# Block 1 of a linear-attention and SwiGLU kernel: its q turned by VectorE, its sums of h put off behind the next pair

## The chip, the cores and the metric

The kernel runs on one core of a Trainium2 chip. The metric is the time of one execution in device microseconds (us). In the profiles PE is TensorE (PEld is its weight load), DVE is VectorE, ACT is ScalarE, POOL is GpSimd and SP is SyncE, whose queue issues most of the DMAs.

## The reference

```python
q, k, v: (8, 8, 576, 64)        # batch, heads, sequence, head_dim, float32
kv  = einsum('bhsd,bhse->bhde', k, v)
out = einsum('bhsd,bhde->bhse', q, kv)
out = out / sqrt(mean(out * out, axis=-1) + 1e-6) * g_norm
x   = out.transpose(0, 2, 1, 3).reshape(4608, 512)
y   = (silu(x @ w_gate) * (x @ w_val)) @ w_out     # w_gate, w_val: 512 x 1536, w_out: 1536 x 512
```

The three weights arrive as 64-bit words, and the kernel rounds them to float32 itself.

## The kernel before

**Blocks.** The 4608 tokens are cut into nine blocks of 512 (BLK), and the loop over n takes one block at a time. `Att` makes a block's x: kv from k and v (`load_kv`, `kv`), q loaded and turned so that the head dimension lies on the partitions (`load_q`, `turn`, `turn_q`), the product of q and kv (`product`), the root (`root`), the scaling (`scale`), and x turned back (`turn_x`). `Ffn` multiplies it with the weights: `up` gives h, `down` multiplies h with w_out. The attention of block n + 1 runs in between the products of block n's `down`, by the table that `steps` returns.

**Fast matrix products.** All products but the first block's up go by a scheme with seven products of half-size matrices in place of eight (Strassen's in Winograd's form). Its products are numbered 1 to 7, and `multiply(p)` issues product p and then the additions in `after<p>`. They gather in PSUM banks: 1, 6, 7 and 4 in "b", 2 in "a", 5 and then 3 in "c" (`CHAIN`). `after7` adds bank "c" to the copy u3 on DVE; only when that is read may product 3 add into the same bank. PSUM has three buffers of "b", two of "c" and "m" and one of "a".

**The blocks differ.** Block 0 has a plain up (`plain_up`, line 1008), because the weights are still being loaded and rounded. Block 1's up is one level deep (`Up`, six pairs j of 128-wide column groups, line 551): each pair takes three differences of weights, made by POOL in `prepare` into buffers of the pool "t" (nine of them, 256 KB each). From block 2 on (DEEP) up is two levels deep (`Inner`, line 706), and its weight sums, the leaves, come from DRAM. Block 1 makes these leaves besides its own work: after each product `make(4)` takes up to four steps of `leaf_steps`, which are small DVE additions and, in between, DMAs on SP that write t buffers, r buffers and the one buffer xi to the DRAM tensors w. A t buffer comes free for POOL only when such a write has landed.

**Sums of h.** Products 5 and others of `down` need sums of h's quarters: `h_sums(j, k, engine)` makes s1 = a21 + a22 and then a21 = s1 - a11, in place in h. In block 0 `plain_end` makes them for all six pairs in two large DVE instructions (128x1536 elements). In block 1 `after3` of pair j makes them for that pair (128x256), behind two POOL multiplications that write h.

**Order of pairs in block 1.** `Up.sequence` interleaves a pair with the one before it, which it calls last: 1, 5, then 4 and 3 of last, then 6, 2, 7. So `after3` of pair j comes after product 3 of pair j, which runs between products 5 and 6 of pair j + 1; `after7` of pair j + 1 comes at that pair's end.

**q.** From block 3 on (TURNED) q is loaded by `load_quarters`: 32 DMAs put the 32-column quarters of each head on their own partitions, so that DVE's transpose of 32x32 squares (line 331) turns it. Before that, q is loaded in rows of 256 bytes and turned by PE in 16 transposes per block (line 337), copied from PSUM by ACT and DVE. Block 1's q lands in four t buffers, block 2's in two buffers of the pool "ld" (four of them, which also hold k, v and the raw weights).

**Around the change, in block 0.** After `plain_end` PE has the kv products of block 1, the 16 transposes of its q, product 1 of block 0's down, block 1's first q product, product 5, product 6, and so on. POOL makes nine differences of w_out (`turn_t`, line 112) in t buffers for products 5, 7 and 4. The order on every engine comes from a list scheduler that follows the order of the program and the dependences; `tc.issue_after(x)` holds what is issued within it behind instruction x in that order. Each engine, and SP's queue, works through its list in order.

Of the kernel before, what the change touches and what calls it, by code (L numbers as in the profile page):

```python
# [8 lines left out]
F32 = mybir.dt.float32  # L9
# [5 lines left out]
P = 128  # L15
# [3 lines left out]
def kernel(  # L19
# [41 lines left out]
    nc = tc.nc  # L61
# [5 lines left out]
    BLK = P * T  # L67
# [5 lines left out]
    NP = NF // 2  # L73
    KT = 9
    LD = 2 * KT * D
# [4 lines left out]
    def pool(name, bufs, **kw):  # L80
        return ctx.enter_context(tc.tile_pool(name=name, bufs=bufs, **kw))

    consts = pool("consts", 1)
    ld_pool = pool("ld", 4)
# [26 lines left out]
    add = lambda e, o, a, b: e.tensor_tensor(out=o, in0=a, in1=b, op=OP.add)  # L111
# [3 lines left out]
    def ring():  # L115

        return r_pool.tile([P, 4, BLK], F32, name="r")

    class Words:
# [12 lines left out]
        def __init__(self, src, shape):  # L132
            self.raw = ld_pool.tile([P, LD], U32, name="ld")[:, 0 : 2 * BLK]
            dst = self.raw.rearrange("p (a b) -> p a b", a=shape[0])
            self.sent = nc.sync.dma_start(out=dst, in_=src)
            self.shape = shape
            self.begun = False
# [55 lines left out]
    class Att:  # L193


        def __init__(self, n):
            self.n = n

            self.cut, half = divmod(n, 2)
            self.split = half * D  # L200
            self.ps, self.z = {}, None
            self.q, self.k, self.v, self.room = [], {}, {}, None
            self.halves = []

        def parts(self, t):

            n, first = self.n, P * t - D * self.n
            if t < self.cut:
                return [(n - 1, S + first, 0, P)]
            if t == self.cut and self.split:  # L210
                return [(n - 1, S - D, 0, D), (n, 0, D, P)]
            return [(n, first, 0, P)]
# [73 lines left out]
            self.q.append(ld)  # L286

        def load_q(self, i):
            if self.n >= TURNED:
                self.load_quarters(i)  # L290
                return
            if self.n == 1:
                tiles = [t_tile().rearrange("p a b -> p (a b)") for _ in range(2)]
            else:
                ld = ld_pool.tile([P, LD], F32, name="ld")
                tiles = [ld[:, 0:BLK], ld[:, BLK : 2 * BLK]]
            for t in range(2):
                tile_ = tiles[t].rearrange("p (h d) -> p h d", h=H)
                for b, s0, p0, p1 in self.parts(2 * i + t):
                    nc.sync.dma_start(  # L300
                        out=tile_[p0:p1], in_=q[b, :, s0 : s0 + p1 - p0, :].rearrange("h p d -> p h d")
                    )
                self.q.append(tile_.rearrange("p (j u) d -> p j (u d)", u=2))
# [21 lines left out]
        def turn_q(self, i, pools=None):  # L325

            if i == 0:
                self.qt = ring().rearrange("p j (t c) -> p t j c", t=T)
            if self.n >= TURNED:
                to = self.qt[:, :, 2 * i : 2 * i + 2].rearrange("p t j c -> p j t c")  # L330
                nc.vector.transpose(out=to.rearrange("p j t c -> p (j t c)"), in_=self.q[i])
                return
            for t in (2 * i, 2 * i + 1):
                pool = pools[t % 2] if pools else m_psum
                ps = pool.tile([P, NS, P], F32, name=pool.name[0])
                for j in range(NS):
                    nc.tensor.transpose(ps[:, j], self.q[t][:, j], ident)
                if t % 2 if self.n == 0 else t:
                    self.copied_q = nc.scalar.copy(out=self.qt[:, t], in_=ps)
                else:  # L340
                    nc.vector.tensor_copy(out=self.qt[:, t], in_=ps)
# [186 lines left out]
    TURNED = 3  # L528
# [44 lines left out]
    class Up(Quad):  # L573
# [25 lines left out]
        def after7(self):  # L599
            self.u3 = self.piece(2)  # L600
            copied = nc.scalar.copy(out=self.u3, in_=self.ps["b"])

            with tc.issue_after(copied.ins):
                nc.scalar.activation(out=self.s, in_=self.s, func=ACT.Silu)
            add(nc.vector, self.u3, self.ps["c"], self.u3)

        def after4(self):
            g = self.piece(3)
# [3 lines left out]
        def after3(self):  # L612
            add(nc.vector, self.u2, self.ps["c"], self.u2)
            mul(nc.gpsimd, self.h[:, :, 0:HB], self.s, self.u2)
            self.ffn.ended = self.ffn.h_sums(self.j, 1, nc.vector)

        def multiply(self, p):
            super().multiply(p)
# [183 lines left out]
    def t_tile(key=None):  # L802

        stream.held.append(key)
        return t_pool.tile([P, 2, 2 * P], F32, name="t")
# [114 lines left out]
    class Ffn:  # L920
        def __init__(self, n, att):
            self.n, self.att = n, att
            self.h = h_pool.tile([P, NF, BLK], F32, name="h")
            self.ps, self.leaf_room, self.ended = {}, None, None

            self.making, self.later, self.latest = [], [], []

# [45 lines left out]
        def down(self, nxt):  # L973

            down = self.down_
            fill = nxt.steps() if nxt else {}
            for p in (1, 6, 5, 7, 2, 4, 3) if 5 in fill else (1, 5, 6, 7, 2, 4, 3):
                if p == 1:
                    down.turn_t(7, self.ended)
                if p == 6:  # L980
                    down.turn_t(4, nxt.halves[0] if nxt and nxt.n >= TURNED else None)
                down.multiply(p)
                self.make(12)
                if p == 5 and self.n == DEEP - 1:
                    for i in range(2):
                        self.loads(i)
                if p in fill:
                    fill[p]()
                if p in (1, 7) and self.latest:

                    with tc.issue_after(nxt.scaled.ins):
                        for step in self.latest.pop(0):
                            step()
                if p == 1:
                    down.turn_s3()

# [57 lines left out]
    for n in range(NB):  # L1056
        ffn = Ffn(n, blocks[n])
        nxt = blocks[n + 1] if n + 1 < NB else None
# [84 lines left out]
```

## Time and profile before

| | us |
|---|---|
| median of 8 runs (1035.22 to 1036.97) | 1035.71 |
| the profiled execution | 1035.98 |
| its span, first to last instruction | 1034.2 |
| PE busy | 1014.4 |
| PEld busy | 904.7 |
| DVE busy | 695.9 |
| POOL busy | 368.5 |
| ACT busy | 231.9 |
| granted TensorE clock, share of full | 1.00 |

The stages by PE's lines: attention of block 0 to about 35 us; block 0's plain up to 114; kv products, transposes of q and block 0's down to 160; block 1's up to 240; block 1's down to 282; then two-level blocks. Line 111 is the helper `add`, 112 `sub`, 113 `mul`, so these are read by their tiles (h, s, xi, t, r). In a timeline row the columns are start, duration, engine, line, operation, output and input tile with shapes, count, and in brackets the idle time before it with what ended it. A row of waits has the sum, the number and the longest. A row of the chain has start, duration and who carried it.

### The profile page before, as it was taken

Reading aid. Unit: us, or ns where it says so; the run is one execution under the profiler, and the core shown is the slowest. Engines: PE = TensorE matmul, PEld = TensorE weight load, DVE = VectorE, ACT = ScalarE, POOL = GpSimd, SP = SyncE. Lnnn points to the kernel's source line nnn. Section 1 sums busy time; section 2 is a strip of 40 time slices with the busy share of each in tenths; the row PEclk is TensorE's granted clock in tenths of the full one; section 3 lists DMA queues with packets and bytes.
Section 4 is the critical chain, followed back from the end, with each engine's and each line's share of the span. In section 5 each row is a group of like instructions: output and inputs, shape, how many; then the busy total and the mean of one; then the engine's idle time right before and its main releaser. Section 6 shows DMA issues by size and latency. Waiting matters only on the chain.

```text
span 1034.2 us, 21447 instructions
## 1 busy us (share of the span) xinstructions
PE 1014.4 (98%) x8586; PEld 904.7 (87%) x8586; DVE 695.9 (67%) x1184; ACT 231.9 (22%) x362; POOL 368.5 (36%) x280
## 2 busy tenths in 40 slices
PE   5999999999999999999999999999999999999998
PEld 4544688878899989998999899988999899989997
DVE  2999596886756855586666666674669466856661
ACT  2765121122221211212111112111212111211110
POOL 0000443334025612463156305640455136513670
PEclk9999999999999999999999999999999999999999
DMA  8689704773678457855686468736862766067601
GB/s 221 204 258 268 138 1 127 188 200 84 192 207 249 101 120 211 242 140 113 182 247 169 66 202 242 198 54 183 239 197 52 168 196 193 22 159 212 189 29 42
DMA packets 247876, 168.15 MB, mean 163 GB/s; under 512 B 124640, under 2 KB 215904, under 8 KB 247776
## 3 DMA queue, kind: packets, MB, share of 16 engines
q1 hardware_dynamic: 221280, 163.36, 57.7%
q10 hardware_dynamic: 26432, 3.41, 2.1%
q8 instruction: 68, 1.11, 0.4%
q14 instruction: 32, 0.26, 0.1%
q0 software_dynamic: 64, 0.00, 0.0%
HBM read 138.02 MB, written 22.41 MB: 155 GB/s over the span
## 4 chain that ended last, share of the span: by engine, by line
PE 90%; DVE 5%; DMA 3%; issue 1%; SPq 1%; ACT 1%; DVEq 0%; ACTq 0%
PE b L706 26%; PE b L551 20%; PE c L706 13%; PE c L551 9%; PE a L706 6%; PE a L551 5%; PE b L1008 4%; PE c L1008 4%; PE m L316 1%; PE m L357 1%; DVE r L112 1%; DMA h<-in_v_dram 1%; DVE xi L112 1%; DVE t L111 1%; DVE r L111 1%
## 5 line engine op out<-in xcount | busy, mean ns | idle before, releaser
L111 POOL TENSOR_TENSOR r<-r 128x256 f32<-128x256 f32 (+1 forms) x105 | 110.9, 1063 | 310.4 <-DVE r L111 263.1
L111 DVE TENSOR_TENSOR r<-b,r 128x512 f32<-128x512 f32 (+1 forms) x273 | 162.1, 606 | 64.9 <-PE b L706 59.6
L112 POOL TENSOR_TENSOR t<-wo 128x512 f32<-128x512 f32 x81 | 115.4, 1449 | 193.5 <-DVE wo L111 104.7
L111 DVE TENSOR_TENSOR r<-c,r 128x512 f32<-128x512 f32 (+1 forms) x179 | 108.5, 618 | 94.7 <-PE c L706 55.5
L706 PE MATMUL b<-x,t 128*128 128x128 f32 x1092 | 151.1, 275 | 0.0
L706 PEld LDWEIGHTS b<-x,t 128*128 128x128 f32 x1092 | 136.5, 192 | 0.7 <-DVE r L111 0.2
L111 DVE TENSOR_TENSOR r<-a,r 128x512 f32<-128x512 f32 (+1 forms) x99 | 62.5, 631 | 106.6 <-PE a L551 62.9
L706 PE MATMUL c<-xi,t 128*128 128x128 f32 x840 | 112.2, 275 | 0.4 <-DVE xi L111 0.4
L113 POOL TENSOR_TENSOR h<-r 128x1024 f32<-128x1024 f32 (+1 forms) x40 | 81.2, 2046 | 82.6 <-DVE r L111 77.1
L706 PEld LDWEIGHTS c<-xi,t 128*128 128x128 f32 x840 | 102.8, 192 | 0.5 <-DVE xi L111 0.5
L551 PE MATMUL b<-wo,h 128*128 128x256 f32 x432 | 99.4, 382 | 0.1
L551 PE MATMUL b<-t,h 128*128 128x256 f32 x432 | 96.9, 381 | 0.0
L551 PEld LDWEIGHTS b<-t,h 128*128 128x128 f32 x432 | 81.3, 190 | 11.3 <-issue 0.2
L551 PEld LDWEIGHTS b<-wo,h 128*128 128x128 f32 x432 | 79.9, 190 | 12.7 <-DVE h L113 2.5
L720 ACT COPY r<-b 128x512 f32<-128x512 f32 x63 | 36.9, 586 | 212.1 <-PE b L706 205.3
L706 PE MATMUL b<-xi,t 128*128 128x128 f32 x588 | 79.9, 276 | 0.0
L706 PEld LDWEIGHTS b<-xi,t 128*128 128x128 f32 x588 | 72.4, 192 | 0.1
L706 PE MATMUL b<-x,wg 128*128 128x128 f32 x336 | 52.7, 279 | 0.2 <-DVE x L112 0.2
L706 PE MATMUL b<-x,wv 128*128 128x128 f32 x336 | 51.3, 275 | 0.0
L551 PE MATMUL c<-t,s 128*128 128x256 f32 x216 | 48.3, 380 | 0.0
L551 PE MATMUL a<-wo,h 128*128 128x256 f32 x216 | 48.3, 379 | 0.0
L551 PE MATMUL c<-wo,h 128*128 128x256 f32 x216 | 48.1, 379 | 0.0
(136 smaller groups left out, 1573.8 us busy)
## 6 DMA issues: line engine op xcount, KB each, us to landing
t<-w SPq DMA_DIRECT2D x336, 256.0 KB, 3.5
out_dram<-r SPq DMA_DIRECT2D x17, 512.0 KB, 3.1
ld<-in_k_dram SPq DMA_DIRECT2D x26, 288.0 KB, 4.7
ld<-in_v_dram SPq DMA_DIRECT2D x26, 288.0 KB, 5.6
ld<-in_moe_w_gate_dram SPq DMA_DIRECT2D x12, 512.0 KB, 4.8
ld<-in_moe_w_val_dram SPq DMA_DIRECT2D x12, 512.0 KB, 4.7
ld<-in_moe_w_out_dram SPq DMA_DIRECT2D x12, 512.0 KB, 4.7
w<-t SPq DMA_DIRECT2D x18, 256.0 KB, 2.5
```

The source lines that it names most:

```text
L111: add = lambda e, o, a, b: e.tensor_tensor(out=o, in0=a, in1=b, op=OP.add)
L112: sub = lambda e, o, a, b: e.tensor_tensor(out=o, in0=a, in1=b, op=OP.subtract)
L113: mul = lambda e, o, a, b: e.tensor_tensor(out=o, in0=a, in1=b, op=OP.mult)
L316: nc.tensor.matmul(self.kv_ps[r][u * D : (u + 1) * D, g, :], lhsT=k[:, u, c, :], rhs=v[:, u, c, :], start=(c == 0), stop=(c == KT - 1),)
L357: self.multiplied = nc.tensor.matmul(self.ps[i][u][p : p + D, t, j, :], lhsT=self.qt[rows, 2 * i + t, j, p : p + D], rhs=kvs[b % 3][rows, ...
L551: nc.tensor.matmul(banks[e][:, e], lhsT=lhsT, rhs=rhs, start=first and i == 0 and (e == 0 or banks[0] is not banks[1]), stop=i == self.ste ...
L706: nc.tensor.matmul(ps[:, i, f], lhsT=self.weight(o, p, f), rhs=self.operand(o, p), start=first and (i, f) == (0, 0), stop=True, skip_group ...
L720: nc.scalar.copy(out=dst, in_=ps)
L1008: nc.tensor.matmul(t, lhsT=w[f // 2][:, i, P * (f % 2) : P * (f % 2 + 1)], rhs=x[:, i, of], start=(i == 0), stop=(i == NS - 1),)
```

## The change

Two edits in block 1 (n == 1) and what keeps the order around them. Its q is loaded by `load_quarters` into two ld buffers and turned by two DVE transposes, which stand behind block 0's sums of h in program order; the subtraction `turn_s3` of block 0's down is held behind them, and products 5 and 6 of block 0's down behind block 1's q products. In block 1's up `after3` of pairs 0 to 4 no longer makes the sums of h: it leaves them owed, and `after7` of the next pair makes them behind its addition. The last pair makes them in `after3` as before.

```diff
@@ class Att
+            self.quarters = n == 1 or n >= TURNED
...
         def load_q(self, i):
-            if self.n >= TURNED:
+            if self.quarters:
                 self.load_quarters(i)
                 return
-            if self.n == 1:
-                tiles = [t_tile().rearrange("p a b -> p (a b)") for _ in range(2)]
-            else:
-                ld = ld_pool.tile([P, LD], F32, name="ld")
-                tiles = [ld[:, 0:BLK], ld[:, BLK : 2 * BLK]]
+            ld = ld_pool.tile([P, LD], F32, name="ld")
+            tiles = [ld[:, 0:BLK], ld[:, BLK : 2 * BLK]]
...
         def turn_q(self, i, pools=None):
-            if self.n >= TURNED:
+            if self.quarters:
                 to = self.qt[:, :, 2 * i : 2 * i + 2].rearrange("p t j c -> p j t c")
-                nc.vector.transpose(out=to.rearrange("p j t c -> p (j t c)"), in_=self.q[i])
+                self.q_turned = nc.vector.transpose(out=to.rearrange("p j t c -> p (j t c)"), in_=self.q[i])
                 return
...
@@ class Up, after7
-            add(nc.vector, self.u3, self.ps["c"], self.u3)
+            added = add(nc.vector, self.u3, self.ps["c"], self.u3)
+
+            owed, self.ffn.owed = self.ffn.owed, None
+            if owed:
+                with tc.issue_after(added.ins):
+                    owed()
...
@@ class Up, after3
-            self.ffn.ended = self.ffn.h_sums(self.j, 1, nc.vector)
+            if self.j < NP - 1:
+                self.ffn.owed = lambda: self.ffn.h_sums(self.j, 1, nc.vector)
+            else:
+                self.ffn.ended = self.ffn.h_sums(self.j, 1, nc.vector)
...
@@ class Ffn, down
-                down.multiply(p)
+                with tc.issue_after(nxt.multiplied.ins) if self.n == 0 and p in (5, 6) else ExitStack():
+                    down.multiply(p)
...
                 if p == 1:
-                    down.turn_s3()
+                    with tc.issue_after(nxt.q_turned.ins) if self.n == 0 else ExitStack():
+                        down.turn_s3()
```

More of the change, by code (lines that the diff above doesn't have):

```diff
@@ L923, in __init__ @@
             self.h = h_pool.tile([P, NF, BLK], F32, name="h")
-            self.ps, self.leaf_room, self.ended = {}, None, None
+            self.ps, self.leaf_room, self.ended, self.owed = {}, None, None, None
             self.making, self.later, self.latest = [], [], []
```

## The prediction

> **What bounds the kernel now.** I read the page's busy shares and its chain first, then the waits of PE, then the timelines of DVE, POOL and SP around them.
>
> ```profile
> PE 1014.4 (98%) x8586; PEld 904.7 (87%) x8586; DVE 695.9 (67%) x1184; ACT 231.9 (22%) x362; POOL 368.5 (36%) x280
> ...
> PE 90%; DVE 5%; DMA 3%; issue 1%; SPq 1%; ACT 1%; DVEq 0%; ACTq 0%
> ```
>
> PE is busy for 98% of the span and carries 90% of the chain, so only two things shorten the run: work taken off PE, and PE's idle time. The list of PE's waits holds one idle item inside the stretch that is changed:
>
> ```profile
> PE c L551 <- DVE r L111: 3.5, 3, 1.7
> ```
>
> That is three stalls in block 1's up, each of a product 3 that waits until VectorE has read the bank "c" (after7's addition). The timeline of PE dates them:
>
> ```profile
> 200.71 1.99 PE L551 MATMUL c<-x,wv 128*128 128x256 f32 x8 [1.67 <-DVE r L111]
> 215.13 1.99 PE L551 MATMUL c<-x,wv 128*128 128x256 f32 x8 [0.66 <-DVE r L111]
> 228.64 1.99 PE L551 MATMUL c<-x,wv 128*128 128x256 f32 x8 [1.15 <-DVE r L111]
> ```
>
> **First edit, q of block 1.** It takes 16 transposes off PE, and they are on the chain, between the kv products and product 1 of block 0's Down:
>
> ```profile
> 116.72 0.59 PE c L337 x4
> 117.30 0.44 PE b L337 x4
> 117.74 0.44 PE c L337 x4
> 118.18 0.44 PE b L337 x4
> 118.61 5.18 PE b L551 x24
> ```
>
> 0.59 + 3 x 0.44 = 1.9 us, ending when product 1 starts, at 118.61. The three ACT copies and one DVE copy that went with them (0.6 to 0.7 us) lie beside PE and are worth nothing. Product 1 reads h[:, :, 0:HB] of the even parts, which the sums of h don't write, so it starts at 116.72 and ends at 121.90.
>
> What comes instead is two stream transposes on DVE, queued behind the sums of h. Their price is in the later blocks, in the instructions of line 331:
>
> ```profile
> L331 DVE STREAM_TRANSPOSE r<-ld x12: 1223/1230/1235, 345.5 to 887.5; 128x1024 f32<-128x1024 f32 x12
> ```
>
> The sums of h, in DVE's timeline, end at 118.82:
>
> ```profile
> 115.27 1.76 DVE L111 TENSOR_TENSOR s<-h 128x1536 f32<-128x1536 f32 x1
> 117.06 1.76 DVE L112 TENSOR_TENSOR h<-s,h 128x1536 f32<-128x1536 f32 x1
> ```
>
> So far the transposes would end at 121.3, before product 1 does, and 1.9 us would be kept. But POOL's timeline shows a cover that goes away:
>
> ```profile
> 107.51 6.16 POOL L112 TENSOR_TENSOR t<-wo 128x512 f32<-128x512 f32 x5 [104.65 <-DVE wo L111]
> 117.39 6.26 POOL L112 TENSOR_TENSOR t<-wo 128x512 f32<-128x512 f32 x4 [3.72 <-PE c L337]
> ```
>
> Of its nine subtractions of wo, four stand still for 3.72 us because their t buffers hold q until PE has turned it. With q in ld buffers they run on from 113.67 at 1.23 us each, into the sums of h. What that costs is seen elsewhere: the four that met the second sum took 6.26 us, 1.3 more than 4 x 1.23, and at 132.91 two DVE instructions that take 1.28 us alone took 3.43 beside POOL (one POOL instruction ahead of each). So the first sum waits until 116.13 (two subtractions after 113.67), 0.86 us; the second waits for one more, 1.23 us; the sums end at 120.9. The transposes at 345.46 and 349.06 kept 1.23 and 1.22 us beside a busy POOL, so I hold them up by nothing: they end at 122.1 and 123.3. The order of PE's instructions in the new kernel puts four matmuls of the second half of q behind eight of the first, so PE stands from 121.9 to 123.3 but for these eight. The rest of the 1.09 us that this product takes (123.80 to 124.89) ends near 124.3: the net gain is 0.6, not 1.9. DVE's next steps (turn_s3, 1.76 us, to 125.1 and the reduction that started at 125.62) come 0.5 to 0.6 earlier as well; they run without a gap up to the scaling that ends 0.46 us ahead of PE's turn at 148.42, so that slack stays. Bounds: 1.9 if POOL does not get in between, 0 if it gets in between once more (1.23 would end the second transpose at 124.5 and the product at 125.5; DVE and PE then lose 0.6, which I add to the range).
>
> The loads: five DMAs become 32, issued on SP at the same place, 97.95. A whole block's quarters elsewhere:
>
> ```profile
> 346.72 16.61 SPq L280 DMA_DIRECT2D ld<-in_q_dram  x32
> ```
>
> 0.52 us each, landing 2.1 us after issue. Each waits for the DMA eight before it (so the list of the built kernel's waits), and the first eight queue behind the k and v loads of 92 to 98, where landing took up to 8.7 us. I take 104 for those eight, then 24 x 0.52 = 12.5 and 2.1: 118.6. The second transpose can't start before 122.1, so 3.5 us are spare. Queued behind on SP are only k and v of block 2, now issued near 117 instead of 106.9 and first read at 180.
>
> The Trainium skill, "DMA: Bandwidth & Descriptors", section Specifications, speaks against the new load: it wants 512 B or more in a piece for line rate, and here the pieces have 128 B; its section Bandwidth gives 0.68 to 0.95 us for DMAs of 4 to 64 KB, so that 32 in a row would be an estimated 22 to 30 us, the last at 120 to 128, and at the far end PE would lose about 5 us, so that the whole change would cost 3 instead of gaining. This trace has that load at 16.6 us, with the DMA share at only 0.4 in its stretch (60 GB/s, yet not full), and I go by the trace.
>
> **Second edit, the sums of h in block 1's up.** Two small DVE instructions per pair (0.34 us each alone) move from behind after3 to behind the next after7. They cost the same there. What goes is their wait for POOL:
>
> ```profile
> DVE h L112 <- POOL h L113: 8.7, 4, 3.1
> ```
>
> The first such wait, on POOL and then on DVE:
>
> ```profile
> 192.99 1.27 POOL L112 TENSOR_TENSOR t<-wg,wv 128x512 f32<-128x512 f32 x1 [3.18 <-DMA w<-t]
> 194.22 1.27 POOL L113 TENSOR_TENSOR h<-r 128x512 f32<-128x512 f32 x1
> ```
>
> ```profile
> 195.51 1.47 DVE L112 TENSOR_TENSOR h<-s,h 128x256 f32<-128x256 f32 x1 [2.90 <-POOL h L113]
> ...
> 198.64 0.68 DVE L112 TENSOR_TENSOR xi<-wg 128x512 f32<-128x512 f32 x1
> ...
> 199.97 0.68 DVE L111 TENSOR_TENSOR r<-c,r 128x512 f32<-128x512 f32 x1
> ```
>
> POOL waits for a transfer that frees a t buffer, then multiplies h; DVE idles 2.90 us, its addition at 199.97 is late, PE stands 1.67. Does PE get these back? Three things say not all. (1) In the idle time POOL ran two instructions, which now meet DVE, about 1.05 us each: a wait of 2.9 is worth 0.8 to 0.9, and that of 3.07 about 1. (2) DVE is itself the tighter engine: in 205.54 to 219.95 it worked a whole pair without a wait and took 14.4 us, 9.3 of its own and some five POOL instructions of 1; PE needs 12.25 for a pair, 13.7 with the kv products. (3) What is late next: the write xi<-wg at 198.64 must wait until the transfer of the pair before has left xi. It was issued at 192.16 to 192.98, in the stretch where q of block 2 fills the queues (DMA share 0.94 to 1.24 from 186 to 196):
>
> ```profile
> w<-xi SPq DMA_DIRECT2D x1, 384.0 KB, 5.1
> ```
>
> It lands between 197.3 and 198.1; today the 2.90 us hide that.
>
> In the time base of before: DVE reaches that write near 195.2 and waits to 197.5; 1.33 us of its own follow up to the addition, which ends at 199.55. PE was ready at 199.04, so it stands 0.55 instead of 1.67: 1.1 gained. Up to the next stall nothing changes in DVE's work, both engines are 1.1 earlier, and the 0.66 stays. From the third addition to the fourth DVE took 13.51 with 3.07 idle; 10.44 + 2 = 12.4 against PE's 12.36: the 1.15 goes. Together 1.1 + 1.15 = 2.25. Bounds: 3.5 if all three vanish; 1.0 if the transfer lands at 198.6 (PE at 200.6) and DVE carries 0.2 to 0.3 more from each pair to the next.
>
> The sums owed by pair 4 now fall at 236.6, beside block 2's copy of q, and the last pair's end at 243.4 as now; product 5 of Down reads them at 247.64. They cost nothing with 4 us of cover.
>
> **Sum.** 0.6 + 2.25 = 2.85 us. The profiled execution took 1035.98 for a span of 1034.2, so I expect a span near 1031.3; that execution is 0.27 above the median of 1035.71, which goes to 1032.9.
>
> **Rivals.** *All of it:* POOL slips behind the sums and no transfer is in the way: 1.9 + 3.5 = 5.4, 1030.3. For it: each stall named above really ends when its DVE line ends. Against it: every POOL instruction that met such a DVE line in this trace held it. *Nearly nothing:* the next thing late (xi's transfer, then DVE's 14.4 us a pair) keeps the first two stalls whole and the first edit gives 0: only the last stall's 1.15 goes, 1034.6, and anything from 2.1 gained to none counts here. For it: DVE shows no idle time in 195.5 to 221. *Slower:* the quarters land late because only eight are in flight. With landing time L their end is 98 + 32 x L/8 + L; for the 5.7 us that k loads take it is 126.5, the second transpose ends at 127.7, the product at 128.7 instead of 124.9: 3.8 lost against 2.25, 1037.3. It decides from a last landing of 122.1; all gain is gone at 125, an L of 5.4. Against it: the backlog of k and v drains, and alone L is 2.1. That the change doesn't do what it says can be set aside: the new order on DVE and PE shows the transposes and sums where the text puts them.
>
> **How the numbers follow.** A measurement here can tell about 0.2%, 2.1 us. Forecast (gain 2.1 to 4): 0.55, its own range 1031.7 to 1033.6. All of it: 0.12. Nearly nothing: 0.26. Slower: 0.07, of that 0.06 over the bound. Faster 0.67, same 0.27, slower 0.06. The range goes from 1030.6, most of the first rival, to 1035.2, which leaves the worse half of the second and the third out.
>
> **What the profile after would show.** Right: no transposes of q between the kv products and Down's product 1; POOL's nine subtractions in one run to about 121; the sums of h near 2 us later; two transposes of 1.23 and a gap of about 1 us on PE ahead of the q product; DVE's waits for POOL h gone from block 1's up, a DMA wait or none before xi<-wg; PE's stalls on "c" near 1.2 in sum. Wrong: stalls of 3 us still there or a new one elsewhere (bank "b" by a late ACT copy), transposes of over 1.3 us, or quarters that land after 122.

## The result and the profile after

The changed kernel takes 1031.47 us (median of 10 runs, 1030.50 to 1032.09). The kernel before, run beside it, takes 1035.93 (28 runs). The ratio is 0.9957, with a 95% interval of 0.9949 to 0.9965: 4.5 us less, 0.43%, more than the 0.2% that a measurement can tell. Ratios here are of fast executions: one of the five of the changed kernel run again took 2705.46 us and is not in its ratio. The forecast was 1032.9. The result lies inside the range of 1030.6 to 1035.2, and 0.2 below the likeliest case's own range (1031.7 to 1033.6), towards the rival "all of it" (1030.3).

The page of the changed kernel, busy time and then the shares of the chain:

```profile
PE 1013.0 (98%) x8570; PEld 903.5 (88%) x8570; DVE 703.3 (68%) x1185; ACT 230.3 (22%) x359; POOL 371.8 (36%) x280
...
PE 92%; DVE 4%; DMA 2%; issue 1%; ACT 1%; SPq 0%; DVEq 0%; ACTq 0%
```

PE has 16 instructions less and is 1.4 us less busy, while the span fell by 4.4 (1034.2 to 1029.8). So most of the gain is idle time of PE that went, and PE's part of the chain rose from 90 to 92%.

**First edit.** The chain after, from the kv products of block 1 to product 5 of block 0's Down (start, length, what; the 16 x 4 small q products between them are left out):

```profile
115.03 2.27 PE m L314 x144
117.30 5.38 PE b L549 x24
...
123.07 0.23 PE b L355 x8
123.31 0.03 issue
...
124.26 1.92 PE c L549 x8
```

The four rows of transposes of q between the kv products and product 1 of Down are gone. The q products (line 355) now reach from 122.68 to 124.26. VectorE's timeline shows why they take that long, POOL's what met it, and SP's when the quarters were issued:

```profile
115.86 1.85 DVE L111 TENSOR_TENSOR s<-h 128x1536 f32<-128x1536 f32 x1
117.74 2.71 DVE L112 TENSOR_TENSOR h<-s,h 128x1536 f32<-128x1536 f32 x1
120.37 1.23 DVE L329 STREAM_TRANSPOSE r<-ld 128x1024 f32<-128x1024 f32 x1
122.03 1.25 DVE L329 STREAM_TRANSPOSE r<-ld 128x1024 f32<-128x1024 f32 x1 [0.43 <-DMA ld<-in_q_dram]
```

```profile
108.68 14.13 POOL L112 TENSOR_TENSOR t<-wo 128x512 f32<-128x512 f32 x9 [105.82 <-DVE wo L111]
```

```profile
99.97 20.30 SPq L281 DMA_DIRECT2D ld<-in_q_dram  x32
```

The same row in two narrower windows, and the largest of SP's waits in the first of them:

```profile
99.97 7.21 SPq L281 DMA_DIRECT2D ld<-in_q_dram  x8
...
107.22 13.05 SPq L281 DMA_DIRECT2D ld<-in_q_dram  x24
```

```profile
SPq L281 <- DMA ld<-in_k_dram: 1.9, 2, 0.9
```

POOL's nine subtractions run in one piece, as foreseen, to 122.8 rather than 121. The sums of h took 1.85 and 2.71 instead of 1.76 and 1.76: POOL held them for 0.09 and 0.95 us. The second transpose waited 0.43 us for the last quarter. The 32 DMAs began 2.0 us later than assumed and took 20.3 us on SP. The first eight took 7.21 of that, 4.2 of them in waits for loads of k and v issued ahead (1.9, 1.2 and 1.1 in SP's list); the other 24 took 0.54 us each, near the assumed 0.52.

**Second edit.** PE's waits for bank "c" in block 1's up, and DVE's for POOL in the same stretch (total, times, longest):

```profile
PE c L549 <- DVE r L111: 0.7, 1, 0.7
```

```profile
DVE h L112 <- POOL h L113: 1.4, 1, 1.4
```

Before, the first list had 3.5 us in three stalls and the second 8.7 us in four. PE's timeline dates the one stall that is left; it is the middle one:

```profile
212.98 1.99 PE L549 MATMUL c<-x,wv 128*128 128x256 f32 x8 [0.73 <-DVE r L111]
```

The first of the three is not wholly gone; what is left is too short for the list. PE's rows around it, before and after:

```profile
197.16 1.89 PE L551 MATMUL b<-x,t 128*128 128x256 f32 x8
200.71 1.99 PE L551 MATMUL c<-x,wv 128*128 128x256 f32 x8 [1.67 <-DVE r L111]
202.54 1.89 PE L551 MATMUL b<-x,wv 128*128 128x256 f32 x8
```

```profile
196.53 1.89 PE L549 MATMUL b<-x,t 128*128 128x256 f32 x8
198.49 1.99 PE L549 MATMUL c<-x,wv 128*128 128x256 f32 x8
200.32 1.89 PE L549 MATMUL b<-x,wv 128*128 128x256 f32 x8
```

Eight matmuls of this kind that wait for nothing start 1.73 us behind the eight before. After the change product 3 started 1.96 behind its predecessor, and the next product 1.83 behind product 3: 0.34 us are left. Counted in this way the three stalls cost 1.93, 0.93 and 1.42 us before, each 0.26 or 0.27 more than its idle time in the list, and 0.34, 0.99 and 0 after: 4.28 against 1.33.

**Where the 4.4 us lie.** Differences of PE's start times in the traces: the kv products (line 314 or 316), product 5 of block 0's Down (c x24), product 1 of block 1's Down (b x24), and the last c product. The rows from the third on are the experiments below; "changed, again" is the same kernel in a later run.

| trace | kv products to product 5 | product 5 to next Down | from there to the last c | span |
|---|---|---|---|---|
| before | 10.45 | 116.47 | 783.94 | 1034.2 |
| changed | 9.23 | 113.53 | 783.51 | 1029.8 |
| q alone | 9.16 | 115.84 | 783.04 | 1032.1 |
| sums alone | 10.44 | 113.05 | 783.15 | 1030.2 |
| sums ahead of the addition | 9.31 | 115.89 | 783.29 | 1032.6 |
| POOL held | 9.19 | 121.31 | 783.71 | 1037.3 |
| quarters on two queues | 8.89 | 113.68 | 783.31 | 1029.2 |
| changed, loads put off | 8.98 | 113.29 | 783.69 | 1028.7 |
| changed, loads as before | 8.98 | 113.28 | 783.04 | 1028.9 |
| two queues and loads put off | 8.74 | 113.40 | 783.33 | 1028.4 |
| changed, again | 9.11 | 113.53 | 784.25 | 1029.9 |

The first edit gave 1.22 us and the second 2.94, which is, to 0.01, what the three stalls lost by their starting times. Against them stands 0.59 that the profiled execution lost ahead of the kv products, where PE waits at the start for v of block 0 (4.0 us before, 4.6 here, 4.0 again when the changed kernel ran a second time); that differs between executions of one kernel. The other 0.8 lies behind block 1, where the changed kernel's own two traces differ by 0.74.

### The profile page after: what moved, and what is told of

It is laid out like the page before. It is cut to its first block, busy times and chain, and to the rows that moved or that the text cites. A ratio compares the mean times of both kernels' runs of the same rounds, so it can differ in the third digit from the quotient of the medians.

```text
span 1029.8 us, 21440 instructions
## 1 busy us (share of the span) xinstructions
PE 1013.0 (98%) x8570; PEld 903.5 (88%) x8570; DVE 703.3 (68%) x1185; ACT 230.3 (22%) x359; POOL 371.8 (36%) x280
## 4 chain that ended last, share of the span: by engine, by line
PE 92%; DVE 4%; DMA 2%; issue 1%; ACT 1%; SPq 0%; DVEq 0%; ACTq 0%
PE b L712 26%; PE b L549 21%; PE c L712 13%; PE c L549 10%; PE a L712 6%; PE a L549 5%; PE b L1018 4%; PE c L1018 4%; PE m L355 1%; PE m L314 1%; DMA h<-in_v_dram 1%; DVE xi L112 1%; DVE r L112 1%; DVE r L111 1%; DMA w<-xi 0%
```

## The experiments

### Each edit alone

```diff
 # e1_q_only: the sums of h stay where they were
-            if self.j < NP - 1:
-                self.ffn.owed = lambda: self.ffn.h_sums(self.j, 1, nc.vector)
-            else:
-                self.ffn.ended = self.ffn.h_sums(self.j, 1, nc.vector)
+            self.ffn.ended = self.ffn.h_sums(self.j, 1, nc.vector)
```

> The first edit alone: block 1's q in quarters, turned by VectorE; the sums of h stay in after3 as before. Theory (the two edits add up, and each works in its own stretch): from the kv products of block 1 to product 5 of block 0's down 1.2 us less than before (9.2 us instead of 10.45), PE's stalls on bank c in block 1's up still near 3.5 us in sum, ratio to before about 0.9988. Rival 1 (what the sums of h wait for depends on where q lies, since q no longer takes four t buffers): the stalls fall below 2 us here already. Rival 2 (the first edit gives nothing at the end, it only shifts the wait): ratio 1.000.

Measured: 1033.40 us, ratio 0.9977 (0.9967 to 0.9986). The first stretch is 9.16, 1.29 less than before; the sums of h took 2.33 and 2.70 and the transposes ran without a wait. PE's waits:

```profile
PE c L549 <- DVE r L111: 2.8, 2, 1.7
```

The first stretch came out as forecast; the time did not: 0.9988 lies outside the interval. Two of the three stalls stay at their sizes (1.68 and 1.15). The middle one of 0.66 fell out of the list (0.28 is left by starting times) without any change in that code, which is the 0.63 in the second stretch. The first of VectorE's rows in that pair that differs, in the kernel before and here:

```profile
205.87 1.51 DVE L112 TENSOR_TENSOR wv<-wv 128x256 f32<-128x256 f32 x1
```

```profile
205.66 0.41 DVE L112 TENSOR_TENSOR wv<-wv 128x256 f32<-128x256 f32 x1
```

Both start 80.97 to 80.98 us behind product 5 of Down, and a POOL subtraction (t<-wg,wv) starts 0.02 to 0.03 ahead of them in both (205.84 and 205.64). Before, VectorE was held; here POOL was (1.56 us for 1.27). Why the tie falls this way when q leaves the t buffers is not shown; in the sums-first kernel below, which has the same order, it fell the same way.

```diff
 # e2_sums_only: block 1's q loaded and turned as before
-            if self.quarters:
+            if self.n >= TURNED:
                 self.load_quarters(i)
...
-                with tc.issue_after(nxt.multiplied.ins) if self.n == 0 and p in (5, 6) else ExitStack():
-                    down.multiply(p)
+                down.multiply(p)
```

> The second edit alone: sums of h owed to the next pair's after7; block 1's q loaded in rows and turned by TensorE as before. Theory: PE's stalls on bank c fall from 3.5 us to 0.7 us, VectorE's waits for POOL's h from 8.7 us to near 1.4 us, block 1's up 2.9 to 3.0 us shorter, ratio about 0.9972. Rival (the transfer out of xi is late next, as the prediction had it): the first stall stays at 0.5 us or more and the gain is 2.2 us, ratio 0.9979.

Measured: 1032.05 us, ratio 0.9966 (0.9954 to 0.9979). The first stretch is as before (10.44), the second 113.05, 3.42 less; one stall of 0.6 is left, the middle one. VectorE waited 0.5 us for w<-xi and the first stall is gone all the same, so the rival fell. The second edit is worth about 3 us, then, and the first about 1.3. They do not quite add up (1.92 + 3.42 against 4.16 in the first two stretches). By starting times 0.79 of the 1.18 too much lies in the middle stall, which is smaller with either edit alone (0.28 and 0.85) than with both (0.99), and 0.32 in the first, which is gone with the sums alone and not with both.

### Sums ahead of the addition

```diff
 # e6_sums_first, in after7
-            added = add(nc.vector, self.u3, self.ps["c"], self.u3)
...
-                with tc.issue_after(added.ins):
-                    owed()
+            done = owed() if owed else None
+            with tc.issue_after(done.ins) if done else ExitStack():
+                add(nc.vector, self.u3, self.ps["c"], self.u3)
```

> The changed kernel with the owed sums of h ahead of after7's addition on VectorE instead of behind it. If the waits for POOL were what cost, they are gone here too and only two instructions of 0.34 us each (with at most two POOL collisions) come ahead of the addition: PE's stalls on bank c rise from 0.7 us to 1.4 to 2.5 us, ratio 0.9965 to 0.9975. If the place behind the addition is what pays, the stalls are back at 3 us or more, ratio 0.9985.

Measured: 1033.91 us, ratio 0.998 (0.997 to 0.9989); stretch 115.89 in block 1, stalls 2.9 in two. The edit does not put the sums ahead of the addition. Without the hold behind the addition the scheduler puts the owed sums where the kernel before has them: VectorE's order is that of the first edit alone, instruction for instruction. DVE's timeline shows the old wait:

```profile
190.23 0.41 DVE L111 TENSOR_TENSOR s<-h 128x256 f32<-128x256 f32 x1
...
195.60 1.47 DVE L112 TENSOR_TENSOR h<-s,h 128x256 f32<-128x256 f32 x1 [2.96 <-POOL h L113]
...
200.05 0.69 DVE L111 TENSOR_TENSOR r<-c,r 128x512 f32<-128x512 f32 x1
```

It is a second measurement of the first edit, then, and it shows that the hold behind the addition is what works in the second edit; writing the sums later in the program does nothing. What they would cost ahead of the addition was not measured.

### POOL kept away from the sums of h

```diff
 # e4_pool_held: POOL's six last subtractions behind the transposes of q
-                    down.turn_t(7, self.ended)
+                    down.turn_t(7, nxt.q_turned if self.n == 0 else self.ended)
```

> The changed kernel with POOL's differences for products 7 and 4 of block 0's down held until q of block 1 is turned, so that POOL is idle while VectorE makes block 0's sums of h. Theory A (q's last quarter, landing near 122.0, is what the second transpose waits for): the sums of h end 0.9 us earlier, the first transpose too, the second still starts when q has landed; the stretch from the kv products to product 5 stays at 9.2 us within 0.1. Theory B (POOL's collisions are what costs): that stretch falls to 8.8 us.

Measured: 1039.29 us in one run, span 1037.3, 7.5 more than the changed kernel. DVE's timeline, with the root of the norm behind it:

```profile
118.84 1.24 DVE L329 STREAM_TRANSPOSE r<-ld 128x1024 f32<-128x1024 f32 x1
121.51 1.25 DVE L329 STREAM_TRANSPOSE r<-ld 128x1024 f32<-128x1024 f32 x1 [1.43 <-DMA ld<-in_q_dram]
...
125.78 1.01 DVE L373 TENSOR_SCALAR z<-z 128x16 f32<-128x16 f32 x1
126.82 1.20 DVE L376 TENSOR_SCALAR y<-z 128x16 int32<-128x16 int32 x1
128.05 1.19 DVE L383 SCALAR_TENSOR_TENSOR a<-y 128x16 f32<-128x16 f32 x1
```

The sums ran in 1.76 each. Counted from the kv products (114.55 here), the first transpose began at 4.29 instead of 5.34, yet the second at 6.96 instead of 7.00, since it waited 1.43 for the quarters, and the first stretch stayed at 9.19, as theory A said: with POOL out of the way the landing binds. POOL's six subtractions started at 122.83 and met five small DVE instructions of the root, three of them shown, which take 0.17 us alone and took 1.01 to 1.20 here. Counted from the kv products, the first half's scaling came 4.85 us later than in the changed kernel, and the second half's 6.0, since POOL also met the weight sums in between at other places (2.1 us more, less 1.0 in the second root). PE paid:

```profile
PE m L402 <- DVE r L113: 5.8, 2, 5.5
```

The 5.5 is the wait for the second scaling, at 153.03. It cost more than itself. Three rows of windows, one ahead of the wait and two behind it (busy time of PE, PEld, DVE, ACT and POOL, then the granted clock, the DMA share and GB/s):

```profile
142.00:147.00 5.00, 5.00 (x25) 4.41 (x24) 5.00 (x4) 0.58 (x1) 4.25 (x3) 1.00 0.00 0
...
153.00:155.00 2.00, 1.97 (x9) 2.00 (x10) 2.00 (x3) 0.69 (x1) 0.00 (x0) 0.50 0.00 0
155.00:162.00 7.00, 7.00 (x27) 5.88 (x27) 3.40 (x5) 0.96 (x2) 2.69 (x3) 0.79 0.00 0
```

PE's granted clock was 0.50 behind the idle time and 0.79 after that; the eight transposes took 1.94 us instead of 1.04 and the product behind them 6.73 instead of 5.18. 5.5 + 0.9 + 1.55 is about the 7.8 by which the second stretch grew. POOL's collisions with the long sums cost 1.0 to 1.7 us; the same instructions moved past them cost 5.5 of waiting and 2.4 at a lower clock.

### Quarters of q on two queues

```diff
 # e3_two_queues, in load_quarters
-                            nc.sync.dma_start(
+                            queue = nc.scalar if self.n == 1 and r % 2 else nc.sync
+                            queue.dma_start(
```

> The changed kernel with half of block 1's quarters (the odd strips, 16 of the 32 DMAs) issued by ScalarE instead of SyncE. Theory A: the quarters' last landing binds the second transpose of q (it waited 0.43 us for it, start 122.03), since SP needed 0.63 us for each of 32 issues. With two issuers the last landing comes some 8 to 10 us earlier, the wait of 0.43 goes, and the stretch from the kv products to product 5 of Down falls from 9.23 to about 8.8 us: time 1031.1. Theory B: the landing is not what binds, because POOL's nine subtractions get in at another place when the transposes shift, or because ScalarE's 16 issues (about 10 us of its time) put off the last silus of block 0 and with them the last sums of h. Then the stretch stays at 9.2 or grows by up to 1.5 us: time 1031.5 to 1033.

Measured: 1031.13 us, ratio 0.995 (0.9936 to 0.9964). DVE's timeline:

```profile
111.21 1.25 DVE L330 STREAM_TRANSPOSE r<-ld 128x1024 f32<-128x1024 f32 x1 [2.46 <-DMA ld<-in_q_dram]
...
115.66 2.51 DVE L111 TENSOR_TENSOR s<-h 128x1536 f32<-128x1536 f32 x1
118.20 2.70 DVE L112 TENSOR_TENSOR h<-s,h 128x1536 f32<-128x1536 f32 x1
120.83 1.23 DVE L330 STREAM_TRANSPOSE r<-ld 128x1024 f32<-128x1024 f32 x1
```

The first half of q landed early enough for the scheduler's place ahead of the sums, the wait of the second is gone, and the first stretch is 8.89 us, near the 8.8 of theory A. SP's last issue ended at 115.21 instead of 120.27, 5 us earlier and not 8 to 10. Two things changed at once, the landing and the place of the first transpose, and the run does not separate them. The whole time can't be told from the changed kernel's.

### What became of the transfer of xi

The forecast kept 0.55 us of the first stall, since xi<-wg would have to wait for the store w<-xi. In the changed kernel VectorE did not wait for it, and 0.34 us of the stall were left by starting times. The chain of the changed kernel dates the store, from issue to landing:

```profile
190.25 4.65 DMA w<-xi
```

It had landed at 194.90, while VectorE, held by POOL, was busy up to the addition at 195.81 that stands ahead of xi<-wg. SP's order had changed as well: one load of block 2's q had moved ahead of the stores. Two kernels were to put it back.

```diff
 # e8_old_sp_order (e9_loads_as_before: behind stream.sent[1 + i], the second and third such stores)
                 if nxt.n < TURNED:
-                    for i in range(2):
-                        nxt.load_q(i)
+                    with tc.issue_after(stream.sent[6].ins):
+                        for i in range(2):
+                            nxt.load_q(i)
```

> The changed kernel with one thing put back: block 2's first q loads are held behind the store w<-xi ahead of them, so that SP issues in the order of before (both q loads behind it), while DVE's order stays that of the changed kernel. Theory A (the prediction's step of 0.55 us failed because the sums owed also moved a q load ahead on SP, so that the second w<-xi was issued at 190.25 and had landed when xi<-wg wanted its buffer at 196.42): that store is issued up to 1.0 us later, DVE waits up to 0.5 us ahead of xi<-wg, the first stall of PE on bank c near 201 comes back with 0.3 to 0.55 us, and the stretch from product 5 of block 0 to product 1 of block 1's Down grows from 113.53 to about 114.0: time 1031.9. Theory B (the store lands early enough in either order, since DVE reaches it earlier): no wait ahead of xi<-wg, the stretch stays at 113.5, time 1031.5.

Measured: 1030.55 us, ratio 0.9946 (0.9933 to 0.9958). The edit was another than intended: the last store of that kind written at that place is the fifth, so the four loads went to 203.95 and later and no load stood beside the stores. No wait ahead of xi<-wg, second stretch 113.29. It decides nothing about the order.

> The changed kernel with SyncE's order of before around 190 us: both DMAs of block 2's first q load behind the second store w<-xi, the other two behind the third (the kernel with q loads put off instead pushed them behind the fifth, which was another edit than intended). VectorE's and GpSimd's orders are those of the changed kernel. Theory A (the first stall on bank c went wholly only because one q load moved ahead of that store): the store w<-xi is issued up to 1 us later than 66.0 us after product 5 of Down, VectorE waits ahead of xi<-wg, and a stall of 0.3 to 0.55 us of PE on bank c comes back near 201: stretch from product 5 to product 1 of the next Down 113.9 to 114.1 us, time 1031.9. Theory B (with the sums off VectorE's way, w<-xi is issued and lands early in either order): no wait ahead of xi<-wg, the stretch 113.4 to 113.6, time 1031.5 as the changed kernel.

Measured: 1030.88 us, ratio 0.9951 (0.9938 to 0.9965). Here SP's order is that of before. SP's and DVE's timelines:

```profile
190.86 0.80 SPq L822 DMA_DIRECT2D w<-xi  x1
```

```profile
193.72 0.68 DVE L111 TENSOR_TENSOR r<-a,r 128x512 f32<-128x512 f32 x1
196.03 0.69 DVE L112 TENSOR_TENSOR xi<-wg 128x512 f32<-128x512 f32 x1 [1.63 <-DMA w<-xi]
...
197.37 0.69 DVE L111 TENSOR_TENSOR r<-c,r 128x512 f32<-128x512 f32 x1
```

DVE does wait for the transfer, 1.63 us, three times the 0.5 that the theory of the kernel above gave it, and theory B's "no wait" is wrong. Yet PE stands even less there than in the changed kernel:

```profile
196.40 1.89 PE L549 MATMUL b<-x,t 128*128 128x256 f32 x8
198.12 1.99 PE L549 MATMUL c<-x,wv 128*128 128x256 f32 x8
```

Product 3 starts 1.73 us behind the product ahead of it, the spacing without a wait, and the addition ended at 198.06 (197.37 + 0.69), just in time. In the changed kernel it ended at 198.43 (197.75 + 0.68) and product 3 started 0.23 late. The second stretch is 113.28: below theory B's 113.4 to 113.6, and far from theory A's 113.9. So SP's changed order is not why the stall shrank. In the changed kernel POOL held DVE three times on the way (two writes of xi in 2.09, wg in 1.49 and 1.37), here once (wg in 1.43), and the transfer took up the difference.

### Both small gains together, and the changed kernel again

```diff
 # e10_two_queues_late_loads: e3_two_queues and e8_old_sp_order in one
 # e11_after_again: the changed kernel
```

> Both edits that came out below the changed kernel in one: the odd quarters of block 1's q issued by ScalarE, and block 2's q loads put off behind the fifth store w<-xi. If both gains are real and lie in different stretches (0.3 us in the stretch from the kv products to product 5, 0.2 us in block 1's Up), the two stretches read 8.9 and 113.3 us and the time is 1030.3 to 1031.0; if the single runs' 1031.1 and 1030.6 were noise, it is that of the changed kernel run beside it.

> The changed kernel unaltered, on the same chip as the two others of this call, so that gains of a few tenths of a microsecond can be judged against it: 1031.5, both theories. Its trace shows how far the stretches of one kernel differ from run to run: 9.23 and 113.53 us in the first.

Measured: the two edits together 1030.16 us, ratio 0.9949 (0.9937 to 0.9962), stretches 8.74 and 113.40; the changed kernel again 1031.75 us, ratio 0.9955 (0.9942 to 0.9969), stretches 9.11 and 113.53. The first stretch reads 8.98 to 9.31 in the six traces with q turned by VectorE, its load on one queue and POOL not held, and 8.74 and 8.89 with the load on two. Of the 0.4 between the two kernels here, 0.24 is the second queue's, for the loads put off alone gave 8.98. The second stretch is 0.13 shorter with the loads put off, not 0.2. The intervals overlap nearly whole, so the version with both beats the kernel before, but whether it beats the changed one stays open. In the second trace of the changed kernel the sums of h took 2.28 and 2.71 and the second transpose did not wait for a quarter: POOL's phase, and with it the wait of 0.43, differs between executions of one kernel.

## Why the prediction was right, and where its terms were off

The result lies 1.4 us below the forecast. Both edits gave more than their terms: the first 0.62, the second 0.69.

- **PE's 1.9 us of transposes, partly given back: right.** They went, and the gap came back on PE ahead of the q products, because VectorE ends the transposes after product 1.
- **The first edit's net gain was mis-sized: 0.6 forecast, 1.22 measured (1.34 in the second trace, 1.29 alone, 1.14 to 1.47 in six traces).** The term that failed is POOL's hold on the sums: 0.86 + 1.23 = 2.09 us in the text, 0.09 + 0.95 = 1.04 in the first trace, 0.52 + 0.95 = 1.47 in the second. The second sum was held for 0.94 or 0.95 in all six, the first for 0.04 to 0.72. Counted from the kv products, the sums ended at 6.46 in the sum (120.9 - 114.44) and at 5.42 in the trace (117.74 + 2.71 = 120.45, less 115.03). Of this 1.04 the wait for the last quarter took 0.43 back: 0.61 net, which is the whole difference of 0.62. In the first trace, then, two errors of opposite sign met.
- **The loads of q: the price was too low.** The sum let the last one land 4.2 us behind the kv products, with 3.5 us to spare; in the first trace the second transpose could start 7.0 behind them, and nothing was spare. The row of a later block was right for the 24 DMAs (0.54 each for 0.52). What was too small is the wait of the first eight for the loads of k and v ahead of them: the text has them issued by 104, the trace by 107.2 (0.6 of that is this trace's later start). The landing from which the "slower" rival was to decide, 122.1, is 7.7 behind the kv products, 0.7 later than the first trace's. The fear taken from the Trainium skill ("DMA: Bandwidth & Descriptors", Bandwidth) seems to have come near: at the section's lower figure of 0.68 us per DMA the 32 would take an estimated 21.8 us, and 20.30 were measured. But the section's table is for DMAs issued from GpSimd, which the prediction does not say, and the trace's 20.30 are a wait and then 0.54 per DMA, so the nearness is chance.
- **The second edit: 2.25 forecast, 2.94 measured, right in kind.** By starting times the three stalls gave 1.59, -0.06 and 1.42 us, where the text has 1.1, 0 and 1.15. Two things were mis-sized. The text priced a stall by its idle time in the list, and each cost 0.26 or 0.27 more. And the first stall was to keep 0.55 and kept 0.34. The mechanism of that step is real (1.63 us of VectorE's wait for w<-xi in the kernel with the loads as before, 0.5 with the sums alone), but it did not bind in the changed kernel, where POOL held VectorE three times and the store had landed before; and the landing was put too late. The text took the store's issue from before, 192.16, which is 67.27 behind product 5; with the sums out of VectorE's way the stores ahead of it went out sooner and it was issued at 66.73 (190.86 - 124.13) in SP's old order, and at 65.99 (190.25 - 124.26) in the new one. In the old order xi<-wg started at 71.90 behind product 5 instead of 72.6 (197.5 - 124.89), and 0.7 earlier is enough for a stall of 0.55. A step that is freed also frees what it had itself held up: here the next store.
- **That VectorE's freed waits are worth less than they show: right.** 7.3 us of waits for POOL went from the list and PE got 2.9.
- **The rivals.** "Nearly nothing" fell with the first stall. "All of it" fell too: 4.16 of 5.4, with 0.73 of the stalls in the list and 0.7 of the 1.9 left. "Slower" did not come.

## What to carry to other kernels

When a wait is taken away, also move the issue of what that engine feeds, and not only its own next instruction: a transfer dated by the old trace is dated too late. Price a stall by the starting times of the work around it, and not by its idle time alone. Price a row of many small DMAs by the queue that stands ahead of it at its own place, and count a spare of a few microseconds as none. Before moving an idle engine's work away from a long instruction that it disturbs, look at what stands behind it: a run of many short instructions pays far more for the same disturbance, and a long idle time of PE can cost more than its length.

## What the runs showed of the hardware that was not expected

- When POOL's subtractions of 1.23 to 1.27 us (128x512) met a row of small VectorE instructions, one of POOL's got in ahead of each, and the short instructions paid as much as long ones: with POOL's six subtractions moved, five DVE instructions of 0.17 us took 1.01 to 1.20 each, where a sum of 1.76 us took at most 2.71. What counts is how many such DVE instructions POOL meets, not how long they are.
- Not every DVE instruction was held. Beside the same nine POOL subtractions in the changed kernel the two stream transposes took 1.23 and 1.25 us and the multiplication h<-h,c, which reads PSUM, 0.69 (at 115.14), as they do elsewhere; beside POOL's six in the kernel with POOL held two reductions took 1.28 together, as without.
- How much POOL holds a given pair of DVE instructions is a matter of phase: the two sums of h took 1.85 + 2.71, 2.28 + 2.71 and, in the kernel with the loads as before, 1.80 + 2.71 us with the same order on both engines.
- Behind an idle time of 5.5 us on PE the granted clock read 0.50 for the next 2 us and 0.79 for the 7 after that, and 1.00 from 162 on (run with POOL held); in the changed kernel it read 1.00 in the same place.
- 32 DMAs of 8 and 56 KB in pieces of 128 B took 20.3 us on SP behind loads of k and v, of which the last 24 took 0.54 each; a later block's 32 took 16.6 us, 0.52 each. Issued half on SP and half on ACT, SP's 16 took 13.21 us, 0.83 each.
